# Sliding-window attention and an MLP on one core: value tiles shifted by half a block, 192 score columns per head in 64x64 tiles, row variance on ScalarE

## The chip, the core and the metric

The kernel runs on one core of a Trainium2 chip. The metric is device time in microseconds (us). The engines are TensorE (PE, its weight loads shown apart as PEld), VectorE (DVE), ScalarE (ACT), GpSimd (POOL, here mostly an issuer of DMAs) and SyncE (SP, an issuer of DMAs).

## What is computed

Eight sequences of 576 tokens with 8 heads of 64 go through causal attention with a window of 128 keys and a linear (ALiBi) bias, and the result, 512 wide, through a row normalisation, a 512 to 2048 to 512 MLP with a ReLU, and a residual add:

```python
scores = scale * np.matmul(q, k.transpose(0, 1, 3, 2))
rel = pos[:, None] - pos[None, :]
mask = (rel >= 0) & (rel < window)                    # window = 128
scores = np.where(mask, scores + bias[None], -1000000000.0)
attn = softmax(scores)
x = heads_joined(np.matmul(attn, v))                  # (8, 576, 512)
mu = np.mean(x, -1); var = np.mean((x - mu) ** 2, -1)
xn = (x - mu) / np.sqrt(var + 1e-06) * g_ln
out = x + np.maximum(xn @ w_ch1, 0.0) @ w_ch2
```

## The kernel before

The 4608 rows are 36 blocks of 128 tokens. Nine blocks make two sequences (a period); r is a block's place in its period, and i its place in the order of work. The blocks with r = 0 are i = 0, 2, 4 and 27: they have no block before them. Eleven chunks of the MLP take 2, 2, 2, 2 and then seven times 4 blocks.

For every block, `attention(i)` does this:

- **Loads.** q, k and v come by DMAs that cast to fp16, issued on POOL's queue (`load_cast`, L496; a block of 128 rows of one operand is one DMA, L551 and L553 are the weights'). The first two blocks come by SP. q and k are turned by SP's transposing DMA into `qkt` (L710), for the first nine blocks by PE (L695).
- **Scores** (`e_s`, L732). The head width of 64 uses half of PE's rows, so two heads run beside each other in 64x128 tiles, into two PSUM banks. Queries of the block meet the keys of the block before (128 columns) and of the block itself (128): 256 columns per head, 16 matmuls a block in 8 pairs, and 8 matmuls where r = 0.
- **Bias and mask.** For i below 5 PE first writes slope times distance into the bank (`e_z`, L748: the scaled identity `sid` times `dist_t`), 8 matmuls of 256 columns, or of 128 where r = 0. Later blocks multiply the exponentials with a table (`mreg`, `mmix`, `mnew`) on DVE (L787).
- **Exponential** on ACT (L780): two instructions of 1024 columns a block, 512 where r = 0.
- **Values** (`e_pv`, L808): per head a matmul of the 128x128 probabilities with the 65 columns of values and ones of the block before, and one with the block's own: 16 matmuls a block, 8 where r = 0. `pva` and `pvb` are the two halves (four heads each).
- **Rows.** DVE divides by the sum (L825, L829), takes mean and variance with bn_stats and bn_aggr (L848, L854), and scales (L868 or L892); the row is turned by PE (L906) for the first six blocks and by SP's DMA afterwards (L921, into `xt`).

The MLP's first product is `A` (L1210, weights `w1sb`), the second `B` (L1247) for the first four chunks; chunks 4 to 10 use a seven-product form of the second matrix product (`seven`, L992, `Pa` to `Pg`), and chunks 9 and 10 of the first one also (`fours`, L1121, `Ua` to `Ug`). ReLUs run on ACT (L1227) or DVE (L1225). Matmuls on `warm_t` (L1287, written ~38 in the order) only keep PE busy at the start.

The order of everything is written out by hand-over of a list: the string `ORDER` names each task with its engine (T for PE, V, A, G, S) and PSUM bank, and every engine works its tasks off in that order. The costs and due times that stand beside the tasks have no effect at run time. So when an instruction waits, all that stands behind it on its engine waits too.

Of the kernel before, what the change touches and what calls it, by code (L numbers as in the profile page):

```python
# [9 lines left out]
FP16 = mybir.dt.float16  # L10
# [46 lines left out]
class Plan:  # L57
# [22 lines left out]
    def run(self):  # L80
# [39 lines left out]
dist:G qs0.0.i:S iden1:G ks0.0.i:S dist01:G dist00:G qs1.0.i:S iden2:G sid5:V sid3:V ks1.0.i:S sid2:V sid0:V sid1:V sid4:V sid7:V sid6:V v0.i:S  # L120
iden3:V ~38 Za0:T0 Zb0:T0 cT0.00:A g.i:A cT0.10:G w0.i:G ~16 T0.0:T0 cT0.01:A q2.i:G eT0.00:V cT0.11:V k2.i:G ~8 Sa0:T0 T0.1:T1 exa0:A v1.i:G eT0.01:A
eT0.10:V Za1:T0 cv0:A G:T2 q3.i:G eT0.11:A k3.i:G Sb0:T0 Gc:A Sa1:T0 exb0:A pva0:T0 v2.i:G Gk:T1 rc0.0:V exa1:A nm0.0:V Zb1:T0 w3.i:G pvb0:T2 Sb1:T0
rc1.0:V nm1.0:V v3.i:G exb1:A mu0:V xs0:V w1.i:G ~10 T2:T0 Z2:T0 w2.i:G ev2:V pvb1:T2 pva1:T3 q5.i:G rc1.1:V S2:T0 rc0.1:V nm1.1:V TX0:T0 exb2:A
nm0.1:V q4.i:G xt0:V exa2:A ~4 T3:T2 mu1:V k4.i:G xs1:V Z3:T0 ev3:A bn1:V w4.i:G TX1:T3 pva2:T0 pvb2:T2 xt1:V S3:T0 Gkc:V rc0.2:V w5.i:G rc1.2:V
A0.0:T3 nm0.2:V exb3:A nm1.2:V w6.i:G A0.12:T1 mu2:V exa3:A xs2:V A0.14:T0 bn0:V r0.12:A r0.0:V pvb3:T2 r0.14:A Z4:T0 rc1.3:V ag0:V pva3:T1 w7.i:G
nm1.3:V A0.2:T3 rc0.3:V nm0.3:V TX2:T0 mu3:V A0.6:T2 xs3:V xt2:A A0.4:T1 r0.6:V k5.i:G bn3:V TX3:T0 r0.4:A A0.8:T2 v4.i:G bn2:V xt3:A ag1:V A0.10:T1
ag2:V k6.i:G r0.8:A A1.14:T0 q6.i:G r0.10:V r0.2:V A1.12:T2 r1.14:A ln0:A T4:T1 rs0:A r1.12:A A1.0:T3 ev4:A q7.i:G A1.4:T0 B1.0:T2 r1.4:V r1.0:V
A1.6:T1 k8.i:G S4:T0 A1.10:T0 exa4:A r1.6:A B0.0:T3 r1.10:A k8.i:G exb4:A B1.4:T2 A1.2:T1 sumT0.0:V B0.4:T3 r1.2:V q8.i:G B1.8:T2 sumT0.1:V k7.i:G
sumT0.2:V B0.8:T3 q8.i:G sumT0.3:V B1.12:T2 q9.i:G T5:T0 o1.0:V B0.12:T3 ev5:A v5.i:G sumT1.0:V pvb4:T1 B2.0:T2 o0.0:V k9.i:G mreg30:A mreg10:A
rc1.4:V mreg11:A pva4:T0 nm1.4:V S5:T0 mreg01:A k10.i:G rc0.4:V nm0.4:V B3.0:T3 exb5:A sumT1.1:V v6.i:G T6:T1 mu4:V exa5:A ag3:V xs4:V q10.i:G A1.8:T0  # L130
ev6:V mreg20:A B3.4:T3 k11.i:G mreg31:A bn4:V mreg21:A ln1:A S6:T0 mreg00:A r1.8:V v7.i:G rs1:A T8:T1 mkb5:V exb6:A dist2:G T7:T0 ev8:V B3.8:T3
q11.i:G exa6:A mka5:V pvb5:T1 q12.i:G ev7:V B2.4:T2 rc1.5:V QT9.i:S nm1.5:V v8.i:G pva5:T0 B2.8:T2 rc0.5:V nm0.5:V k12.i:G mka6:V S7:T0 v8.i:G mu5:V
B2.12:T2 mkb6:V exb7:A QT10.i:S xs5:V v9.i:G TX4:T1 exa7:A B3.12:T3 xt4:V k13.i:G mmixc:V TX5:T0 pva6:T1 o3.0:V xt5:A S8:T0 q13.i:G o2.0:V pvb6:T0
exb8:A A2.2:T3 v11.i:G mkb7:V A2.8:T2 mnewc:V r2.2:A v10.i:G QT11.i:S z2:V mka7:V A2.0:T3 r2.8:A rc1.6:V rc0.6:V z1:V A2.14:T2 r2.0:A nm1.6:V mkb8:V
exa8:A A2.12:T0 nm0.6:V sumT1.2:V pvb7:T3 r2.12:A pva7:T1 bn5:V S9:T0 r2.14:A QT12.i:S rc1.7:V A2.4:T0 z3:V exb9:A ag4:V nm1.7:V A2.10:T2 mu6:V exa9:A
xs6:V A2.6:T3 k15.i:G rc0.7:V bn6:V XT6.i:S r2.4:A mka8:V S10:T0 q15.i:G r2.6:A nm0.7:V B5.0:T0 r2.10:A mu7:V exa10:A ag6:V xs7:V pvb8:T3 pva8:T1
B5.4:T0 ag5:V exb10:A bn7:V XT7.i:S k16.i:G rc1.8:V B4.0:T2 mka9:V k15.i:G nm1.8:V QT13.i:S S11:T0 rc0.8:V dist2a:G nm0.8:V q15.i:G B4.4:T2 mkb9:V
exb11:A v13.i:G bn8:V B5.8:T0 exa11:A mkb11:V q14.i:G pvb9:T3 pva9:T1 ln2:A mka11:V B4.8:T2 rs2:A k14.i:G ag8:V rc0.9:V rc1.9:V B5.12:T0 nm0.9:V
v12.i:G ag7:V nm1.9:V ln3:A B4.12:T2 rs3:A bn9:V k17.i:G mkb10:V pvb11:T1 A3.2:T3 q16.i:G ag9:V o4.0:V ln9:A rs9:A S12:T0 r3.2:A q17.i:G xs8:V
rc1.11:V pva11:T2 o5.0:V XT8.i:S exb12:A A3.0:T3 xs9:V exa12:A A3.4:T0 nm1.11:V XT9.i:S rc0.11:V mka10:V A3.8:T1 r3.4:A nm0.11:V bn11:V A3.6:T0 r3.8:A  # L140
mkb12:V r3.0:A pvb10:T2 pva10:T1 QT14.i:S rc1.10:V S13:T0 rc0.10:V nm0.10:V A3.10:T3 exa13:A nm1.10:V out1.0.i:S bn10:V pvb12:T1 out0.0.i:S r3.6:A
A3.14:T2 ag11:V r3.10:V B6.0:T0 ag10:V r3.14:V ln11:A rs11:A exb13:A A3.12:T3 xs10:V mka13:V XT10.i:S scaleW2:A B7.0:T2 xs11:V r3.12:V B6.4:T0
XT11.i:S scaleW3:V B7.4:T2 scaleW1:A QT15.i:S B6.8:T0 rc1.12:V mkb13:V nm1.12:V B7.8:T2 k19.i:G B6.12:T0 QT16.i:S scaleW0:A v15.i:G S14:T0 o6.0:V
v14.i:G pva13:T3 mka12:V B7.12:T2 out2.0.i:S rc0.13:V exa14:A nm0.13:V pvb13:T1 pva12:T0 o7.0:V A4.8:T3 v20.i:G exb14:A rc1.13:V rc0.12:V nm1.13:V
A4.1:T2 v16.i:G nm0.12:V QT17.i:S mkb14:V S15:T0 r4.1:A v15.i:G mka14:V A4.3:T1 exb15:A bn12:V q18.i:G A4.0:T0 sumT1.3:V exa15:A k18.i:G r4.8:V
A4.10:T2 mka15:V q21.i:G S16:T0 r4.10:A r4.3:V A4.12:T3 q19.i:G exb16:A r4.0:V A4.11:T2 bn13:V q20.i:G exa16:A ag12:V r4.12:V A4.4:T1 dist1:G r4.11:A
mkb15:V k20.i:G A4.9:T0 r4.4:A ag13:V mka16:V v17.i:G ln13:A pvb14:T3 rs13:A A4.15:T2 r4.9:A xs12:V rc1.14:V XT12.i:S nm1.14:V pva14:T1 pva15:T0
rc0.14:V A4.7:T3 nm0.14:V QT18.i:S rc0.15:V nm0.15:V A4.14:T1 r4.7:A xs13:V mkb16:V A4.2:T0 out3.0.i:S bn14:V pvb15:T3 r4.2:A S17:T0 r4.15:A sa4.0:V
A4.6:T0 r4.14:A rc1.15:V sb4.0:V exb17:A A4.5:T2 XT13.i:S nm1.15:V r4.6:A A4.13:T1 bn15:V out6.0.i:S r4.5:A ag14:V sc4.0:V Pa4.00:T3 r4.13:A Pb4.00:T0
QT19.i:S exa17:A sa4.1:V Pa4.01:T3 Pb4.01:T0 ag15:V ln15:A Pa4.10:T3 out5.0.i:S rs15:A Pb4.10:T0 xs14:V out4.0.i:S Pa4.11:T3 xs15:V XT14.i:S Pb4.11:T0  # L150
sb4.1:V pvb16:T2 ra4.0:V k23.i:G pva16:T1 S18:T0 XT15.i:S rb4.0:V k21.i:G Pc4.00:T3 exb18:A Pc4.10:T3 sd4.0:V Pd4.00:T0 v24.i:G rc1.16:V exa18:A
QT20.i:S mka17:V Pc4.11:T3 Pd4.01:T0 k22.i:G rc0.16:V nm1.16:V Pc4.01:T3 mkb17:V Pd4.10:T0 v19.i:G rc4.0:V pva17:T2 Pd4.11:T0 q22.i:G nm0.16:V S19:T0
rd4.0:V Pe4.00:T3 v18.i:G exb19:A sc4.1:V Pe4.10:T3 pvb17:T1 rc0.17:V dist1a:G Pf4.10:T0 q23.i:G rc1.17:V nm0.17:V Pf4.00:T0 sd4.1:V Pe4.11:T3 q24.i:G
Pe4.01:T3 nm1.17:V Pf4.11:T0 k22.i:G QT21.i:S Pf4.01:T0 A5.0:T2 q22.i:G rf4.0:V A5.9:T1 bn17:V v23.i:G r5.0:A re4.0:V exa19:A A5.7:T0 v22.i:G mkb19:V
Pg4.00:T3 q25.i:G r5.9:V S20:T0 bn16:V Pg4.10:T3 k24.i:G exa20:A mka19:V A5.2:T2 v21.i:G mkb18:V Pg4.11:T3 QT23.i:S r5.2:A r5.7:V Pg4.01:T3 k25.i:G
pva19:T1 mka20:V A5.3:T2 rc0.19:V rg4.0:V A5.15:T0 r5.3:A nm0.19:V mka18:V A5.11:T3 r5.15:A ag17:V ag16:V exb20:A QT22.i:S A5.1:T1 r5.11:A pvb19:T2
pvb18:T0 ln17:A rc1.19:V S21:T0 nm1.19:V rs17:A r5.1:A mkb20:V A5.8:T3 xs16:V A5.10:T2 rc1.18:V r5.8:A XT16.i:S pva18:T1 r5.10:A A5.4:T3 rc0.18:V
v26.i:G out7.0.i:S exb21:A nm0.18:V xs17:V A5.14:T2 q26.i:G nm1.18:V exa21:A sa5.0:V A5.6:T1 k26.i:G QT24.i:S r5.14:A sb5.0:V A5.5:T0 r5.6:A bn18:V
r5.4:A A5.13:T2 out9.0.i:S bn19:V XT17.i:S sc5.0:V A5.12:T1 r5.13:A ag18:V mkb21:V Pa5.00:T3 r5.12:A ag19:V Pb5.00:T2 r5.5:V ln19:A S22:T0 rs19:A
sa5.1:V Pa5.01:T3 exb22:A xs19:V Pb5.01:T2 xs18:V Pa5.10:T3 sc5.1:V exa22:A Pb5.10:T2 XT19.i:S sb5.1:V Pa5.11:T3 pva20:T1 ra5.0:V pvb20:T0 XT18.i:S  # L160
# [1169 lines left out]
```

## Time and profile before

| what | us |
|---|---|
| runs shown | 302.86, 299.45, 301.07 |
| median | 301.07 |
| the profiled execution's own time | 300.98 |
| its span, first to last instruction | 299.1 |
| PE busy / DVE / ACT / POOL | 293.3 / 242.8 / 165.3 / 105.4 |
| PE's own waits in all (four) | 2.5 |
| scores L732, 544 matmuls, PE busy (all forms) | 38.2 |
| values L808, 544 matmuls, PE busy (all forms) | 30.4 |
| exponentials L780 on ACT | 67.4 |
| bn_stats L848 and bn_aggr L854 on DVE | 24.2 and 5.7 |

The profiled execution took 300.98 us, 0.09 below the median; 1.9 of it lie around the span. A matmul's time in the profile includes its way through the array (a 65-column matmul is given 193 ns), so neighbours overlap, and what a matmul costs in a row is the distance from its start to the next start.

### The profile page before, as it was taken

To read this page: it belongs to the slowest core of one execution; us is meant where nothing else is said; L and a number is where in the kernel's file an instruction comes from. 1 tells how busy PE (TensorE), PEld (TensorE's weight loads), DVE (VectorE), ACT (ScalarE), POOL (GpSimd) and SP (SyncE) were. 2 spreads that over 40 slices of the span, in tenths; PEclk is the share of its full clock that TensorE was granted. 3 is DMA by queue.
4 is the path that set the end of the run, shared out by engine and by line. 5 is a ranking of instruction groups with operands and counts; after the bars stand their busy time and mean duration, and the time that the engine had idled before them with its cause. 6 is when DMAs were issued, how large, how long until landed. Compare 5 with 4: busy or idle time off the path is not lost.

```text
span 299.1 us, 7458 instructions
## 1 busy us (share of the span) xinstructions
PE 293.3 (98%) x3014; PEld 225.1 (75%) x3014; DVE 242.8 (81%) x583; ACT 165.3 (55%) x273; POOL 105.4 (35%) x138
## 2 busy tenths in 40 slices
PE   8999999999999999899999999999999999999995
PEld 8789756875955578566886588657787799999984
DVE  3397289998879879849978888788899988988983
ACT  3664536794798573368528444676544655245500
POOL 5965369738137428433633567300000000000000
PEclk9799999999999999999999999999999999999999
DMA  6999999999999999999999999968101033012015
GB/s 179 159 196 194 206 144 141 146 138 133 122 219 145 151 224 133 145 140 167 179 166 197 182 159 143 158 171 150 36 19 55 0 125 89 2 37 106 35 55 193
DMA packets 163779, 39.93 MB, mean 133 GB/s; under 512 B 154017, under 2 KB 159137, under 8 KB 163746
## 3 DMA queue, kind: packets, MB, share of 16 engines
q0 software_dynamic: 110000, 17.70, 95.6%
q1 hardware_dynamic: 53744, 21.77, 40.5%
q8 instruction: 23, 0.38, 0.6%
q14 instruction: 10, 0.08, 0.1%
q10 hardware_dynamic: 2, 0.00, 0.0%
HBM read 36.70 MB, written 9.44 MB: 154 GB/s over the span
## 4 chain that ended last, share of the span: by engine, by line
PE 94%; DMA 4%; DVE 1%; ACT 0%; issue 0%
PE fb L1210 32%; PE fb L992 27%; PE fb L1247 9%; PE u L1121 8%; PE sc L732 6%; PE fb L808 6%; DMA qkt<-qk 4%; PE fb L1287 2%; PE sc L748 1%; PE fb L695 1%; PE fb L440 0%; PE fb L906 0%; PE fb L426 0%; DVE ot L1004 0%; DVE xb L829 0%; ACT probs L780 0%
## 5 line engine op out<-in xcount | busy, mean ns | idle before, releaser
L1210 PE MATMUL fb<-xt,w1sb 128*128 128x512 f16 (+1 forms) x576 | 106.4, 332 | 0.6 <-DMA xt<-xs 0.6
L780 ACT ACTIVATE probs<-sc 128x1024 f16<-128x1024 f32 (+1 forms) x72 | 67.4, 975 | 36.0 <-PE sc L732 27.3
L1210 PEld LDWEIGHTS <-w1sb 128*128 128x128 f16 x576 | 61.5, 114 | 27.8 <-DMA xt<-xs 0.9
L1227 ACT ACTIVATE ht<-fb 128x512 f16<-128x512 f32 x88 | 51.1, 598 | 44.4 <-PE fb L1210 44.2
L992 PEld LDWEIGHTS <-ht 128*128 128x128 f16 x560 | 53.2, 98 | 9.2
L496 POOL DMA_DIRECT2D qk<-in_k_dram x38 | 32.8, 866 | 44.3 <-DMA qkt<-qk 36.8
L992 PE MATMUL fb<-w2sb,ht 128*128 128x256 f16 x336 | 44.7, 273 | 0.0
L496 POOL DMA_DIRECT2D qk<-in_q_dram x38 | 32.5, 861 | 16.6 <-DMA qkt<-qk 9.6
L496 POOL DMA_DIRECT2D vx<-in_v_dram x36 | 31.0, 868 | 15.6 <-PE fb L808 12.4
L787 DVE TENSOR_TENSOR probs<-probs,mreg 128x1024 f16<-128x1024 f16 (+1 forms) x46 | 30.4, 667 | 1.1 <-ACT probs L780 1.0
L992 PE MATMUL fb<-ks,ht 128*128 128x256 f16 x224 | 30.8, 273 | 0.0
L1247 PE MATMUL fb<-w2sb,ht 128*128 128x512 f16 x128 | 30.7, 379 | 0.0
L829 DVE SCALAR_TENSOR_TENSOR xb<-fb,rec 128x256 f16<-128x256 f32 x72 | 29.5, 416 | 0.9
L808 PEld LDWEIGHTS <-probs 128*128 128x128 f16 x544 | 23.9, 98 | 6.8
L808 PE MATMUL fb<-vx,probs 128*128 128x65 f16 x496 | 26.1, 194 | 0.0
L1004 DVE TENSOR_TENSOR ot<-fb,xb 128x512 f32<-128x512 f32 (+1 forms) x31 | 19.6, 634 | 6.0 <-PE fb L992 5.6
L848 DVE BATCH_NORM_STATS2 st<-xb 128x6 f32<-128x512 f16 x36 | 24.2, 682 | 0.2
L825 DVE RECIPROCAL rec<-fb 128x4 f32<-128x4 f32 x72 | 12.2, 174 | 14.7 <-PE fb L808 12.4
L1225 DVE TENSOR_SCALAR ht<-fb 128x512 f16<-128x512 f32 x24 | 16.0, 681 | 8.4 <-PE fb L1210 8.3
L1247 PEld LDWEIGHTS <-ht 128*128 128x128 f16 x128 | 11.6, 98 | 11.1
L732 PEld LDWEIGHTS <-qkt 64*128 64x128 f16 x496 | 14.9, 94 | 6.4 <-issue 5.3
L1144 DVE TENSOR_TENSOR ht<-u,probs 128x512 f16<-128x512 f32 x24 | 16.2, 685 | 2.7 <-PE u L1121 1.8
(113 smaller groups left out, 387.7 us busy)
## 6 DMA issues: line engine op xcount, KB each, us to landing
out_dram<-ot SPq DMA_DIRECT2D x32, 256.0 KB, 2.9
qk<-in_q_dram POOLq DMA_DIRECT2D x30, 128.0 KB, 7.6
qk<-in_k_dram POOLq DMA_DIRECT2D x30, 128.0 KB, 7.2
vx<-in_v_dram POOLq DMA_DIRECT2D x28, 128.0 KB, 7.7
w1sb<-in_moe_w_ch_dram POOLq DMA_DIRECT2D x4, 512.0 KB, 9.1
w2sb<-in_moe_w_ch_dram POOLq DMA_DIRECT2D x4, 512.0 KB, 14.1
out_dram<-ot SPq DMA_DIRECT2D x8, 128.0 KB, 1.8
qs<-in_q_dram SPq DMA_DIRECT2D x2, 256.0 KB, 3.6
```

The costliest lines, as they stand in the source:

```text
L496: nc.gpsimd.dma_start(out=dst(p0, n), in_=src[b, :, s0 : s0 + n, :].rearrange("h p d -> p h d"))
L732: nc.tensor.matmul(scs[half][:, g, c0 : c0 + P], kt[rows, 1, hp, :], qkt[i][rows, 0, hp, :], start=not bias, stop=True, skip_group_check=True,
L780: nc.scalar.activation(out=o, in_=n_, func=AF.Exp, scale=inv_sqrt_d)
L787: en.tensor_tensor(out=pv, in0=pv, in1=mask[:, 2 * half : 2 * half + 2, :, lo:], op=ALU.mult)
L808: nc.tensor.matmul(pp[:, hh * (D + 1) : hh * (D + 1) + D + 1], probs[i][:, bank, slot, side * P : side * P + P], vx[i if side else before] ...
L829: nc.vector.scalar_tensor_tensor(out=xb[c][:, j, 256 * half : 256 * half + 256].rearrange("p (h d) -> p h d", d=D), in0=pp[:, :, 0:D], sca ...
L848: nc.vector.bn_stats(out=st[i][:, :], in_=xb[c][:, j, :])
L992: nc.tensor.matmul(o, lhs(f, p), rhs(f), start=first and f == 0 and (p == 0 or key[0] != key[1]), stop=f == F2 - 1, skip_group_check=True)
L1121: nc.tensor.matmul(late[bank][:, FOURTH * f : FOURTH * f + FOURTH], w, rhs[kb], start=first and f == kb == 0, stop=kb == 1, skip_group_che ...
L1210: nc.tensor.matmul(fb[b][:, n_ * x : n_ * x + n_], w1f[f // CB][:, kb, (f + x) % CB, :], xt[c][:, kb, 0:n_], start=(kb == x == 0), stop=(k ...
L1227: nc.scalar.activation(out=o, in_=src, func=AF.Relu)
L1247: nc.tensor.matmul(pm[:, 0 : c1 - c0], ht[c][:, f, j * P : j * P + P], w2sb[f // CB][:, f % CB, c0:c1], start=(f == 0), stop=(f == NFB - 1),)
```

## The change

1. **Value tiles shifted by half a block.** A tile of values now holds the 128 tokens that begin half a block before the queries' block. A query block then needs three pieces of keys: a near tile of 128 keys that all its queries use, and two outer pieces of 64 keys, each used by 64 queries. The score columns per head are 128 + 64 = 192. `load_v` loads tiles in halves where a block's half is not there yet: 42 v transfers on POOL's queue in place of 39, two on SP in place of one, of the same bytes in all. The ring of value tiles has 8 + 6 in place of 9 + 3.
2. **64x64 tiles.** Scores: for each pair of heads four matmuls of 128 columns and four of 64 columns, each with 64 keys as weights and 64 PSUM partitions as target. Where r = 0, two and two. Values: `pw` does the two outer pieces for all heads (16 matmuls, 64 rows by 64 targets, into the two halves of the partitions of one bank), then `pva` and `pvb` do the near tile (4 each, 128x128). `pw` needs the exponentials of both halves.
3. **Bias by matmul** has 192 columns for all blocks, and block i = 27 (r = 0) takes it too instead of a mask. `dist_t` gets a fourth table; POOL makes the tables at the start in 11 steps (before: 3), two of them after the first loads.
4. **Exponentials** 768 columns for every block; masks 768 columns.
5. **Variance.** bn_stats and bn_aggr go. DVE sums each row while dividing (accumulator for all blocks, before for the first 8), makes minus the mean (`mu`, now 36), and ACT squares x - mean with an accumulator (`sq`, 36).
6. **`ORDER` anew.** Among others: PE's `pw` mostly stands beside a score task; of the ReLUs L1225 and L1227, DVE has 45 in place of 24 and ACT 67 in place of 88; 65 matmuls on `warm_t` in place of 76; the weights w3, w1, w2 are issued behind 12 other transfers of POOL (before: w3 behind 7); the first A task follows the scores and values of blocks 0 to 3 and the scores of block 4 (before: the scores of blocks 0 to 3).

```diff
-                        for side in (() if r == 0 else (0,)) + (1,):
-                            for g in range(2):
-                                rows = slice(D * g, D * g + D)
-                                kt = qkt[i if side else before]
-                                c0 = slot * 2 * P + side * P
-                                nc.tensor.matmul(scs[half][:, g, c0 : c0 + P], kt[rows, 1, hp, :], qkt[i][rows, 0, hp, :], ...)
+                        near_ = [(own, lower, upper, 0, 0, P)] + ([(ago, upper, lower, 0, 0, P)] if r else [])
+                        outer_ = [(own, upper, lower, P, HALF, HALF)] + ([(ago, lower, upper, P, 0, HALF)] if r else [])
+                        for g, (kt, keys, to, col, q0, n) in [(g, x) for some in (near_, outer_) for g in range(2) for x in some]:
+                            rows = slice(D * g, D * g + D)
+                            nc.tensor.matmul(scs[half][to, g, c0 + col : c0 + col + n], kt[rows, 1, hp, keys], qkt[i][rows, 0, hp, q0 : q0 + n], ...)
...
-                                scs[half][:, g, slot * 2 * P + lo : slot * 2 * P + 2 * P], sid[:, h, :], dist_t[:, kind, lo:],
+                                scs[half][:, g, slot * W3 : slot * W3 + W3], sid[:, h, :], dist_t[:, kind, :],
...
+        def e_pw(e, b):
+            pr_ = by_head(probs[i])
+            for half in range(2):
+                pp = fb[plan.held[f"V{'ab'[half]}{i}"][1]]
+                for hh in range(4):
+                    h = 4 * half + hh
+                    bank, slot = 2 * half + h % 2, hh // 2
+                    for rows, q_, vt in ((lower, upper, v_after), (upper, lower, v_ago)):
+                        nc.tensor.matmul(pp[q_, hh * (D + 1) : hh * (D + 1) + D + 1], pr_[rows, bank, slot, outer],
+                            vx[VT[vt]][rows, h, 0 : D + 1], start=hh == 0, stop=True, skip_group_check=True)
...
-                    for side in (() if r == 0 else (0,)) + (1,):
-                        nc.tensor.matmul(pp[...], probs[i][:, bank, slot, side * P : side * P + P], vx[i if side else before][:, h, 0 : D + 1], ...)
+                    nc.tensor.matmul(pp[...], pr_[:, bank, slot, near], vx[VT[v_near]][:, h, 0 : D + 1], start=False, ...)
...
-            nc.vector.bn_stats(out=st[i][:, :], in_=xb[c][:, j, :])
-            nc.vector.bn_aggr(out=mv[c][:, j, :], in_=st[i][:, :])
+            nc.scalar.activation(out=squares[:, :], in_=xb[c][:, j, :], func=AF.Square, bias=mean[i][:, 0:1], accum_out=mv[c][:, j : j + 1])
```

More of the change, by code (lines that the diff above doesn't have):

```diff
@@ L124 @@
[L124 to L127, printed above, removed]
@@ L391 @@
         nc.vector.memset(t[:, :, D:VD], 1.0)
+    for n in range(HEADS):
+        nc.vector.memset(vx[VT[n, 0]][0:HALF, :, 0:D], 0.0)
     far = 16000.0
@@ L461, in emit @@
                 )
-            tm.append(add(f"mreg{bank}{slot}", ("ACT", 0.4), emit, d_dist[0], av(MASK_AT, 0.0)))
+            tm.append(add(f"mreg{bank}{slot}", ("ACT", 0.35), emit, d_dist[0], av(MASK_AT, 0.0)))
     tmix, tnew = [], []
@@ L798, in attention @@
         fast = c >= SEVEN
+        n_pair = BLOCK[i] // PERIOD
+        v_near, v_after, v_ago = ((n_pair, r + d) for d in (0, 1, -1 if r else 0))
+        def e_pw(e, b):
[6 more added lines that the diff above has]
+                    for rows, q_, vt in ((lower, upper, v_after), (upper, lower, v_ago)):
+                        nc.tensor.matmul(
+                            pp[q_, hh * (D + 1) : hh * (D + 1) + D + 1],
+                            pr_[rows, bank, slot, outer],
+                            vx[VT[vt]][rows, h, 0 : D + 1],
+                            start=hh == 0,
+                            stop=True,
+                            skip_group_check=True,
+                        )
+        pw = add(f"pw{i}", ("PE", 0.25), e_pw, pr + v_done[v_after, 0] + v_done[v_ago, 1], av(i, 5.0), lat=0.0, acq=[("fb", f"V{x}{i}") for x in "ab"])
+        probs.reads(i, pw)
+        for t in (v_after, v_ago):
+            vx.reads(VT[t], pw)
         for half in range(2):
@@ L835, in e_nm @@
                     op1=ALU.mult,
-                    accum_out=None if fast else sums[i][:, half : half + 1],
+                    accum_out=sums[i][:, half : half + 1],
                 )
@@ L839, in attention @@
             rec.writes(2 * i + half, rc)
-            n_ = add(f"nm{half}.{i}", ("DVE", 0.48), e_nm, [rc], av(i, 5.2 + half), rel=key)
-            if not fast:
-                sums.writes(i, n_)
+            n_ = add(f"nm{half}.{i}", ("DVE", 0.52), e_nm, [rc], av(i, 5.2 + half), rel=key)
+            sums.writes(i, n_)
             rec.reads(2 * i + half, n_)
@@ L1065, in seven @@
                     t, d = plan.transfer(f"out{i}.{cols.start}", "SP", 0.42, 0.8 * (cols.stop - cols.start) / d_model, 0.12, e_d, deps, v0 + (4 * n + 4) * step - 4.0)
-                    ot.reads(k0 + half, d)
+                    ot.reads(k0 + half * (NP - 1), d)
     def first_sums():
-        free = [t for r_ in (probs, qkt) for ts_ in r_.readers.values() for t in ts_] + masked
-        wsums["free"] = free
         for m in range(2):
@@ L1087, in pick1, with tile_reads @@
         return Choice(default, cost)
+    def tile_reads(ring_, n):
+        return [t for k, ts in ring_.readers.items() if k not in ring_.pins and ring_.turn(k) % len(ring_.tiles) == n for t in ts]
     def fours(c, done, v0, room):
@@ L1198, in mlp @@
             return
-        order = [x for n in range(NFB // 2) for x in (n, n + NFB // 2)] if fast else range(NFB)
+        order = [x for n in range(NFB // 2) for x in (n, n + NFB // 2)] if fast and nb == CB else [x for n in range(0, NFB // 2, 2) for x in (n, n + 1, n + NFB // 2, n + NFB // 2 + 1)] if fast else range(NFB)
         two = 2 if nb == 2 else 1
```

491 lines of the change are left out of this document (264 added, 227 removed).

## The prediction

> **What bounds the kernel now.** I read the page's busy shares first, then the list of PE's waits, then busy time by stage, and last the order of time around one block's attention.
>
> ```profile
> PE 293.3 (98%) x3014; PEld 225.1 (75%) x3014; DVE 242.8 (81%) x583; ACT 165.3 (55%) x273; POOL 105.4 (35%) x138
> ```
>
> ```profile
> PE fb L1287 <- DVE warm_t L387: 1.1, 1, 1.1
> PE fb L1210 <- DMA xt<-xs: 0.6, 1, 0.6
> PE sc L732 <- DMA qkt<-qk: 0.5, 1, 0.5
> PE fb L1287 <- DVE xb L829: 0.3, 1, 0.3
> ```
>
> ```profile
> 0.00:20.00 20.00, 18.48 (x234) 15.80 (x235) 9.67 (x53) 10.25 (x15) 14.65 (x26) 0.91 1.37 175
> 20.00:110.00 90.00, 90.00 (x947) 64.46 (x946) 73.72 (x185) 62.55 (x104) 47.64 (x60) 1.00 2.07 162
> 110.00:130.00 20.00, 18.91 (x207) 14.22 (x206) 16.84 (x36) 6.71 (x9) 13.00 (x18) 1.00 2.19 155
> 130.00:210.00 80.00, 80.00 (x833) 56.27 (x832) 66.31 (x158) 47.68 (x77) 30.10 (x37) 1.00 1.68 164
> 210.00:296.00 86.00, 85.91 (x801) 74.32 (x798) 75.93 (x155) 38.08 (x70) 0.00 (x0) 1.00 0.20 60
> ```
>
> PE is the bound and has hardly a hole: its waits add up to 2.5 us, and after the first 20 us it lacks work only in the stage 110 to 130, by 1.1 us, both times for a transposing DMA. It waits for DVE only while the start runs, and for ACT never. So what the change takes from ACT and DVE is worth nothing by itself; only matmul time, the changes of PE's tile shape, the start and the DMA waits count. What they cost is read from starts:
>
> ```profile
> 60.21 0.65 PE L808 MATMUL fb<-vx,probs 128*128 128x65 f16 x16
> 60.78 0.23 PE L732 MATMUL sc<-qkt,qkt 64*128 64x128 f16 x2
> 60.85 0.22 PE L732 MATMUL sc<-qkt 64*128 64x128 f16 x2
> 60.91 0.22 PE L732 MATMUL sc<-qkt,qkt 64*128 64x128 f16 x2
> 60.96 0.22 PE L732 MATMUL sc<-qkt 64*128 64x128 f16 x2
> 61.02 0.22 PE L732 MATMUL sc<-qkt,qkt 64*128 64x128 f16 x2
> 61.07 0.22 PE L732 MATMUL sc<-qkt 64*128 64x128 f16 x2
> 61.13 0.22 PE L732 MATMUL sc<-qkt,qkt 64*128 64x128 f16 x2
> 61.19 0.22 PE L732 MATMUL sc<-qkt 64*128 64x128 f16 x2
> 61.34 0.41 PE L1210 MATMUL fb<-xt,w1sb 128*128 128x256 f16 x2
> ```
>
> Sixteen value matmuls cover 0.65 us, the last one 0.19 of it, so one follows another after (0.65 - 0.19) / 15 = 0.030 us. The last starts at 60.67 and the scores at 60.78: 0.11 in place of 0.03, about 0.09 too long. A pair of score matmuls follows the last after 0.056 us ((61.19 - 60.85) / 6). From the last pair to the next product are 0.15 us, again 0.09 more than 0.056. So a visit to the half-height tiles costs 0.19 us beside its matmuls.
>
> **The change part by part.** The sum is made against the profiled execution's 300.98 us, 0.09 below the median of the runs.
>
> Scores. In a block with r above 0, 8 rounds of 128 columns (8 x 0.056 = 0.448) become 4 rounds of 128 and 4 of 64, each of four matmuls side by side. The trace shows no matmul that writes 64 targets and no four at once. Bounds: four at once cost no more than two do, and a round of 64 columns takes what the value matmul of 65 columns takes, 0.030, so 4 x (0.056 + 0.030) = 0.344; or nothing is gained over pairs, 8 x 0.056 + 8 x 0.030 = 0.688. I take the first, because in the rows above two row halves already work side by side at the price of one. 32 blocks x 0.104 = -3.3 us. Where r = 0, 4 rounds of 0.056 become 4 to 4 x 0.086; I take no change (at most 4 x 0.12 = +0.5).
>
> Values. With r above 0, 16 x 0.030 = 0.48 become 8 near matmuls (0.24) and 8 pairs of outer ones (0.24 if a pair costs one): nothing. The four blocks with r = 0 go from 8 x 0.030 to 0.48: 4 x 0.24 = +1.0. If pairs do not overlap, 36 x 0.24 = +8.6 (a rival below).
>
> Bias matmuls. L748's rows at 14.89 (8 of 128 columns in 0.61 us) and 17.59 (4 of 256 in 0.60) give 0.056 and 0.109 from start to start, so 192 columns lie at 0.082. Before 3 x 8 x 0.056 + 2 x 8 x 0.109 = 3.1 us, after 6 x 8 x 0.082 = 3.9: +0.8.
>
> Changes of tile shape. Counted along the two orders, PE goes into the smaller tiles 37 times before and 44 times after, since most outer value tasks stand next to a score task: 7 x 0.19 = +1.3. If every one stood alone it would be 36 x 0.19 = 6.8.
>
> ACT and DVE. Exponentials: 1023 ns at 1024 columns (64) and 594 at 512 (8) give 809 at 768, so 72 x 0.809 = 58.2 for 67.4. Twenty-one ReLUs leave at 598 ns (-12.6). The square is not in the trace: the nearest row, an ACTIVATE of 512 fp16 elements, takes 626 ns; with DVE's accumulator read of 82 ns on top 0.71, so 36 x 0.63 to 36 x 0.8 = 23 to 29 us. ACT goes to about 167 to 173 us of 299. DVE loses 24.2 + 5.7 (statistics) and 8 (masks: 62 of up to 679 become 60 of 548 ns), gains 28 x 0.210 (means), 56 x 0.082 (accumulators) and 21 x 0.681 (ReLUs): 13 less. All this lies beside PE's matmuls; cost nothing. Were that cover gone, a square that waits for its mean would hold the exponentials behind it on ACT, and through the score banks PE's next scores; but along the new order at least 6.5 us of matmuls lie between scores and their outer value task from block 4 on, against 2 x 0.81 + 2 x 0.55 = 2.7 us of exponentials and masks.
>
> DMAs. Three more value issues on POOL at 0.87 us, same bytes; POOL is 35% busy and waits 46.3 us for q and k tiles to come free, so they are hidden, apart from the start.
>
> The start. PE's first A matmul begins at 19.6 us. The matmuls that stand ahead of it make 14.9 us at full speed, so 4.7 went to waits and to the clock (0.91 over the first 20 us, 1.8 us lost). In the new order 16.8 us stand ahead of the first A, because block 4's turn, bias and scores and block 3's outer values moved forward; with the same 4.7 it begins at 21.5, no loss, as that work is done. Eleven warm-up matmuls fewer are 11 x 0.056 = -0.6. Bounds: the half-clock stretch does not come (-1.8), or a weight comes late (+2.8, a rival below).
>
> The DMA waits of 1.1 us: the transposes of chunk 5's rows are now issued 6.7 us of matmuls ahead of use in place of 8.2, block 21's q and k 14.8 in place of 10.5; one gets worse, one better. No change, bounds -1.1 and +1.5.
>
> Sum: -3.3 + 1.0 + 0.8 + 1.3 - 0.6 = -0.8, so 300.98 - 0.8 = **300.2 us**: the matmul time saved in the scores is given back by four blocks' values, the bias and the tile changes.
>
> **The rivals.**
>
> *The small tiles' weights are not hidden: slower.* Each score block issues 32 weight loads for 0.344 us of matmuls, 16 before for 0.448. Where matmuls are too short to hide a load, the trace shows its price:
>
> ```profile
> 10.41 0.74 PEld L440 LDWEIGHTS fb<-ot 1*128 1x128 f32 x6
> 10.41 0.82 PE L440 MATMUL fb<-ot 1*128 1x1 f32 x6
> ```
>
> one-column matmuls and their loads follow each other after (0.74 - 0.19) / 5 = 0.11 us (the last load itself takes 0.19): 128 columns of fp32 weights. 64 such columns are 0.055 us. At this price a 64-column round costs 0.055, so scores fall back to 0.444 (+3.2) and the outer values to 8 x 0.055 = 0.44 (+0.20 x 36 = 7.2): 310.6. With two bytes a weight loading in half the time, but the two tiles of a row half one after the other, only the scores lose: 303.4. It decides as soon as four loads take longer than 0.030 us. For: no row has a 64-column weight. Against: 128 fp16 columns are hidden behind each 0.030 us value matmul. The Trainium skill, TensorEngine Tiling (Array Packing), section Restrictions, says that column tiling switches the fast weight load off. By that rule the hidden loads of the value rows would not carry over to the new tiles; no run yet shows it. Chance 0.22.
>
> *Outer value pairs do not overlap.* The two matmuls of a pair write the same PSUM bank, in different partitions; the score pairs above write two banks. One after the other they cost 16 x 0.030, +8.6: 308.8. The Trainium skill, same page, section Gotcha 1: PSUM Pressure, says that different row tiles can't access one bank at the same time; the trace has no such pair. Chance 0.10.
>
> *The start and the DMA waits fall well.* No half-clock stretch (-1.8) or no DMA wait in the middle (-1.1): 298.4 with the first, 297.3 with both. For: both hang on moments that the new order shifts. Against: PE still idles while first loads land. Chance 0.22.
>
> *w3 comes late: slower.* POOL issues 12 transfers at 0.87 us ahead of w3, from about 5.5 us on: 16.0, plus the 9.1 us that a w1sb transfer takes to land (median), is 25.1; the second A task needs it at 21.5 + 0.9 = 22.4. +2.8: 303.0. Against: the quickest of the four took 5.8 us, then it is there at 21.8. Chance 0.10.
>
> **How the numbers follow.** The forecast keeps 0.36, as 300.2 with its own range 298.5 to 302.5 (the DMA and r = 0 bounds). A measurement here can tell about 1% from no change: 298.1 and 304.1. Faster: nearly all of the third rival's 0.22 and a little of the forecast's, 0.22. Slower: the second rival, the first's dearer half and a part of combinations, 0.28. Within 1%: 0.50. The range of 8 in 10 runs from 297.0 to 309.0.
>
> **What would show it.** In the profile after: the distance from one block's first score to the next product (0.34 + 0.15 if four tiles overlap, 0.45 or more if weights bound); the 16 outer value matmuls in 0.24 or in 0.48 us; PE's waits still under 4 us in all; the first A near 21.5 us with w3 landed by 22.4; DVE about 229 us busy and ACT about 170 without any change of the time for it. The prediction is wrong if PE waits for ACT or DVE after the start, or if a 64-wide tile costs other than the 128-wide rows suggest.

## The result, and the profile after

The changed kernel is about 1% slower. The first comparison gave 305.05 us against 300.95 for the kernel before, ratio 1.0132 (95% interval 1.0092 to 1.0172); a second one, e1, with seven executions for four, 303.93 against 300.84, ratio 1.0092 (1.0060 to 1.0123). The forecast was 300.2. Ratios leave out disturbed executions, such as the profiled one of the first comparison (377.09 us at a granted clock of 0.76), medians do not; all readings of "after" below are from e1's profile: 303.75 us, span 302.0.

The busy shares of the changed kernel:

```profile
PE 294.7 (98%) x3875; PEld 224.4 (74%) x3875; DVE 229.2 (76%) x620; ACT 168.4 (56%) x323; POOL 108.0 (36%) x148
```

DVE and ACT came out where they were forecast (229, and 167 to 173), and PE is as full as it was. The new forms on ACT, in the list of the costliest groups (count, busy time, mean ns of one, then the idle time before them):

```profile
L824 ACT ACTIVATE probs<-sc 128x768 f16<-128x768 f32 x72 | 55.5, 805 | 33.7 <-PE sc L779 22.8 <-PE fb L874 11.0
L918 ACT ACTIVATE squares<-xb,mean 128x512 f16<-128x512 f16 x36 | 25.9, 721 | 14.1 <-DVE mean L911 13.0 <-DVE rec L889 0.9
L918 ACT ACTIVATION_READ_ACCUMULATOR squares<-xb,mean 128x1 f32 x36 | 6.9, 193 | 0.0
```

An exponential was forecast at 809 ns and takes 805; the square, bounded by 0.63 and 0.8 us, takes 0.72 and 0.19 more to read its sum, so 0.91 in all. The list of PE's waits (us in total, times, longest) has new names behind its first, which is the one that `warm_t` had before:

```profile
PE fb L1346 <- DVE squares L399: 1.1, 1, 1.1
PE fb L1051 <- DVE ot L1063: 1.0, 1, 1.0
PE fb L1269 <- DVE ot L1314: 0.9, 1, 0.9
PE fb L742 <- DMA qk<-in_q_dram: 0.4, 1, 0.4
PE sc L779 <- ACT qktp L752: 0.2, 1, 0.2
PE fb L1269 <- DMA w1sb<-in_moe_w_ch_dram: 0.2, 1, 0.2
```

Both waits of the stage 110 to 130 are gone. One of about 1 us has come in the stage before it and one near 210, as busy time by stage shows (start and end, length, then PE busy; the granted clock is the third number from the end):

```profile
0.00:20.00 20.00, 17.84 (x294) 14.68 (x295) 9.37 (x53) 10.99 (x15) 17.74 (x36) 1.00 1.53 168
20.00:110.00 90.00, 88.96 (x1270) 62.99 (x1269) 65.43 (x187) 61.42 (x121) 47.89 (x59) 1.00 1.76 163
110.00:130.00 20.00, 20.00 (x245) 15.11 (x244) 16.44 (x42) 9.54 (x21) 10.31 (x13) 1.00 1.94 157
210.00:296.00 86.00, 85.06 (x844) 72.97 (x844) 74.60 (x164) 40.34 (x80) 0.00 (x0) 1.00 0.23 63
```

One block's attention in the order of time (start, length):

```profile
118.18 0.24 PE L779 MATMUL sc<-qkt 64*64 64x128 f16 x1
...
118.55 0.43 PE L854 MATMUL fb<-vx,probs 64*64 64x65 f16 x16
118.91 0.61 PE L1051 MATMUL fb<-qs,qs 128*128 128x256 f16 x4
```

From the first score to the first outer value matmul are 0.37 us, from there to the next product 0.36. Neither the weights' price (0.444) nor values one after the other (0.48) is to be seen.

**Where the time went.** Distances from start to start of PE's tasks, summed over both profiles, give this account; what a task takes over the median of its kind, beyond 0.06 us, is put down as a wait:

| us, from start to start | before | after | difference |
|---|---|---|---|
| scores and values | 37.8 | 36.4 | -1.4 |
| the MLP's matmuls (19 of these tasks stand ahead of a small tile before, 35 after, 0.095 each) | 236.6 | 237.9 | +1.3 |
| bias matmuls | 3.2 | 4.7 | +1.5 |
| warm-ups | 6.5 | 6.0 | -0.5 |
| turns of q, k and rows, and gains | 8.0 | 8.5 | +0.5 |
| waits | 2.1 | 3.7 | +1.6 |
| last matmul's start | 295.64 | 298.59 | +2.95 |

In this execution half of the loss is waits and half is work: the small tiles save nothing net and the bias costs more. The forecast had -1.0 for the first two rows together, +0.8 for the bias, -0.6 for the warm-ups and no waits.

**The two new stops.** The stop at 209.7 can be followed through DVE's and SP's rows:

```profile
183.79 20.44 SPq L757 DMA_TRANSPOSE qkt<-qk  x4
204.33 2.86 SPq L978 DMA_TRANSPOSE xt<-xs  x2
```

```profile
208.89 0.41 DVE L949 TENSOR_SCALAR xs<-xb,mean,rstd 128x512 f16<-128x512 f16 x1 [1.12 <-DMA xt<-xs]
...
210.20 0.69 DVE L1063 TENSOR_TENSOR ot<-fb,xb 128x512 f32<-128x512 f32 x1 [0.42 <-DMA out_dram<-ot]
```

The four transposes of the first line end with block 34's. SP can issue that one only at 203.0, because its k lands at 202.9, and is done with it at 204.3; behind it stand the transposes of rows 24 and 25. DVE's next row waits 1.12 us for a buffer that such a transpose still reads (there are three). Behind that row stands `ra7` (L1063), which has to empty PE's bank. So a load on POOL reaches PE through SP and DVE, and PE's list names only the last link.

The other stop is named after DVE, wrongly:

```profile
64.68 4.05 SPq L978 DMA_TRANSPOSE xt<-xs  x2
```

```profile
76.55 1.04 PE L1269 MATMUL fb<-xt,w1sb 128*128 128x256 f16 x8 [0.86 <-DVE ot L1314]
```

The DVE operation that ends just ahead of it comes later in `ORDER`, so this task can't wait for it. It reads block 7's row, whose transpose went out at 67.1 and took 9.3 us: 76.4.

### The profile page after: what moved, and what is told of

Read it like the earlier page. It is cut to its first block, busy times and chain, and to the rows that moved or that the text cites. A ratio compares the mean times of both kernels' runs of the same rounds, so it can differ in the third digit from the quotient of the medians.

```text
span 375.3 us, 9298 instructions
## 1 busy us (share of the span) xinstructions
PE 370.3 (99%) x3875; PEld 250.1 (67%) x3875; DVE 233.7 (62%) x620; ACT 170.1 (45%) x323; POOL 107.9 (29%) x148
## 4 chain that ended last, share of the span: by engine, by line
PE 94%; POOL 2%; DMA 2%; issue 0%; ACT 0%; DVE 0%; POOLq 0%
PE fb L1269 34%; PE fb L1051 30%; PE fb L1306 10%; PE u L1180 8%; PE sc L779 4%; PE fb L874 3%; PE fb L854 3%; DMA qk<-in_q_dram 2%; PE fb L742 1%; POOL qk L517 1%; PE fb L963 0%; PE sc L795 0%; POOL vxp L554 0%; ACT qktp L752 0%; POOL w1sb L609 0%
## 5 line engine op out<-in xcount | busy, mean ns | idle before, releaser
L1269 PE MATMUL fb<-xt,w1sb 128*128 128x512 f16 (+1 forms) x576 | 134.8, 397 | 0.0
L824 ACT ACTIVATE probs<-sc 128x768 f16<-128x768 f32 x72 | 55.5, 806 | 51.5 <-PE sc L779 35.2
L1286 ACT ACTIVATE ht<-fb 128x512 f16<-128x512 f32 x67 | 39.4, 596 | 59.1 <-PE fb L1269 58.7
L1051 PE MATMUL fb<-w2sb,ht 128*128 128x256 f16 x336 | 55.9, 319 | 0.0
L1284 DVE TENSOR_SCALAR ht<-fb 128x512 f16<-128x512 f32 x45 | 30.7, 688 | 36.6 <-PE fb L1269 36.5
L918 ACT ACTIVATE squares<-xb,mean 128x512 f16<-128x512 f16 x36 | 25.9, 719 | 18.2 <-DVE mean L911 16.7
L1063 DVE TENSOR_TENSOR ot<-fb,xb 128x512 f32<-128x512 f32 (+1 forms) x31 | 19.5, 638 | 14.7 <-PE fb L1051 14.5
L832 DVE TENSOR_TENSOR probs<-probs,mreg 128x768 f16<-128x768 f16 x44 | 23.8, 556 | 6.9 <-ACT probs L824 6.8
L1193 ACT ACTIVATE probs<-u 128x512 f32<-128x512 f32 x21 | 12.2, 596 | 26.4 <-PE u L1180 20.2
L1063 DVE TENSOR_TENSOR ot<-fb,ot 128x512 f32<-128x512 f32 (+1 forms) x22 | 14.6, 665 | 14.9 <-PE fb L1051 14.8
L779 PEld LDWEIGHTS <-qkt 64*64 64x64 f16 x992 | 15.9, 111 | 8.1 <-issue 7.3
```

Source lines behind the costliest of these rows:

```text
L779: nc.tensor.matmul(scs[half][to, g, c0 + col : c0 + col + n], kt[rows, 1, hp, keys], qkt[i][rows, 0, hp, q0 : q0 + n], start=not bias, sto ...
L824: nc.scalar.activation(out=o, in_=n_, func=AF.Exp, scale=inv_sqrt_d)
L1051: nc.tensor.matmul(o, lhs(f, p), rhs(f), start=first and f == 0 and (p == 0 or key[0] != key[p]), stop=f == F2 - 1, skip_group_check=True)
L1063: nc.vector.tensor_tensor(out=out[:, p0:p1], in0=src, in1=in1[:, p0:p1], op=ALU.add)
L1269: nc.tensor.matmul(fb[b][:, n_ * x : n_ * x + n_], w1f[f // CB][:, kb, (f + x) % CB, :], xt[c][:, kb, 0:n_], start=(kb == x == 0), stop=(k ...
L1284: nc.vector.tensor_scalar(out=o, in0=src, scalar1=0.0, scalar2=None, op0=ALU.max)
```

## The experiments

Theory A: the miss is the price of the matmuls. Theory B: it is in the queues, transposes and loads that come late. Theory C came up on the way: PE runs short of instructions. Runs that name the same time for the kernel before share its executions. A block count of 31 in two expectations is 30 (block 27 is not doubled).

**e1: the changed kernel again.** No edit.

> The changed kernel once more, unchanged, for a profile at full clock. Theory A (matmul time): the score blocks cost more than 0.344 us or the changes of tile shape more than 0.19 us a visit, so that PE's time after the first 20 us grows by some 4 us without any wait. Theory B (start): the first A matmul begins later than the 21.5 us of the forecast, by 2 to 4 us, and the rest is as forecast. Theory C (DMA waits): PE's listed waits after 20 us add up to 3 us or more, against 1.1 us before. About 304 us in each case.

Result above: A and B each have a part.

**e2: the transposes of rows ahead of those of q and k.**

```diff
-... QT32.i:S ... QT33.i:S ... QT34.i:S ... XT24.i:S ... XT25.i:S ...
+... QT32.i:S ... XT24.i:S ... XT25.i:S QT33.i:S QT34.i:S ...
```

> The changed kernel, but on SP's queue the q and k transposes of blocks 33 and 34 stand behind the row transposes of blocks 24 and 25 and not ahead of them; nothing else moves. Theory B (the miss is in queues): the stop of 1.15 us at 209.7 is a chain: PE waits for DVE's ra7, which stands behind xs, which waits for a buffer that a row transpose still reads, and that transpose stood on SP behind two transposes whose q and k had not landed. Then the stop goes and the time falls by 0.9 to 1.2 us, to 302.8. Rival: the row transposes were late by their own transfers and the next wait of DVE takes the place of this one; the time falls by less than 0.4 us, 303.5 to 304. Theory A (the miss is matmul time) says nothing of this run beyond that the other 2 us stay.

303.18 us against 300.31, 1.0083 (1.0052 to 1.0114). The profiled execution took 301.52 us and has neither stop; block 7's transpose landed 8.2 us after its issue there. One execution without a stop proves little, since e14, of the unedited kernel, has none either. The traces together support the chain: the stop is in none of the seven profiled executions with this order (e2, e7, e10, e11, e15, e16, e18). Of the old order, e1, e13 and e17 have it, with block 34's k landing at 202.9, 201.5 and 202.1 us, and e14 has not, where it landed at 198.4; e6, e8 and e9, whose PE work differs, have none either. The median cannot tell 0.7 us from none, because its executions spread from 301.5 to 304.7, with one at 311.6.

**e3 and e4: the scores issued twice, after and before.**

```diff
-                for half in halves:
+                for half in halves * (1 if bias else 2):
```

> The changed kernel with the score matmuls of the 31 masked blocks with r above 0 issued twice into the same places (the output stays the same). Each block pays the price of its scores once more, without a change of tile shape. Trace price, from the distances of the run above: 0.371 us, 31 x 0.371 = 11.5, 315.4 us. The forecast's price of 0.344: 10.7, 314.6. Rival, weights bound the narrow rounds: 0.444 or more, 13.8, 317.7 or more.

> The kernel before with the same doubling of its 31 masked blocks with r above 0 (output the same): 31 x 0.448 = 13.9, 314.7 us. The difference of the two additions is what the new tiles gain in the scores of these blocks: by the forecast 31 x 0.104 = 3.2 us, by the trace 31 x 0.077 = 2.4 us, and nothing if weights bound the narrow rounds.

e4: 313.6 us against 300.31, 13.3 more; in its trace the doubled blocks take 1.000 where 0.553 stood, so 0.447 a block. e3: 325.94 (321.7 to 328.6), 22 more than e1, far beyond every price. Its trace parts the two causes. Where nothing interferes a doubled block takes 0.721 in place of 0.371 (or 0.824 in place of 0.474 when it leaves the small tiles): the scores cost 0.350, 0.097 less than before, and the forecast's 0.344 was right. The rest is stops of a new name:

```profile
PE sc L779 <- issue: 7.5, 4, 2.5
PE fb L1269 <- issue: 2.7, 2, 2.4
```

```profile
69.14 0.20 PE L779 MATMUL sc<-qkt 64*64 64x64 f16 x2
71.86 0.21 PE L779 MATMUL sc<-qkt,qkt 64*64 64x64 f16 x1 [2.52 <-issue]
```

In the middle of a score task, which waits for nothing, PE stands for 2.7 us. These stops begin ahead of matmuls 990, 1118 and 1246 of the program, 128 apart; with the weight loads that is 256 instructions. A 16 KB transfer on the queue for instructions ends at 63.2, 70.1 and 77.4 us, and PE goes on at 64.8, 71.9 and 78.9.

**e5: the variance on DVE again.**

```diff
-            nc.scalar.activation(out=squares[:, :], in_=xb[c][:, j, :], func=AF.Square, bias=mean[i][:, 0:1], accum_out=mv[c][:, j : j + 1])
+            nc.vector.bn_stats(out=st[i][:, :], in_=xb[c][:, j, :])
+            nc.vector.bn_aggr(out=mv[c][:, j, :], in_=st[i][:, :])
```

> The changed kernel with one part undone: the variance comes from bn_stats and bn_aggr on DVE again, at the places in the order where the squares stood; ACT loses 36 x 0.9 = 33 us, DVE gains 36 x 0.83 = 30 us (229 to about 259, 86% of the span). Theory A and the forecast (ACT and DVE work lies beside the matmuls, its price is nothing): 303.9 within 0.6. Rival (DVE's queue already carries the two stops of the profile, at 75.3 and 209.7, and more work on it makes them longer and adds others): 305 to 308.

311.28 us, 7.4 above e1 (1.0355 to the kernel before, 1.0300 to 1.0411) and above the rival's 308. DVE is 82% busy, about as full as it was before the change (81%), and PE now waits in many places:

```profile
PE sc L780 <- DMA qkt<-qk: 1.8, 1, 1.8
PE fb L1271 <- DMA xt<-xs: 1.1, 2, 0.7
...
PE fb L1053 <- DVE ot L1065: 0.7, 2, 0.4
PE fb L1053 <- DVE ht L1286: 0.7, 1, 0.7
PE fb L1271 <- DVE ht L1286: 0.5, 2, 0.3
```

So DVE's work is not free in this order. It lies beside PE's work only as long as the order was laid for it. PE waits for late results of DVE themselves (`ot`, `ht`) and for transposes of late rows (`xt`); what made the transpose of q and k late (1.8) was not followed.

**e6: half of three in four outer pairs left out** (the oldest keys are missing for three heads in four).

```diff
-                    for rows, q_, vt in ((lower, upper, v_after), (upper, lower, v_ago)):
+                    for rows, q_, vt in ((lower, upper, v_after), (upper, lower, v_ago))[: 1 if hh else 2]:
```

> The changed kernel, its outer value task (16 matmuls of 64x64) leaving out the second matmul of three of the four pairs per half: 10 matmuls in place of 16, so the oldest keys are missing for three heads in four. If the two matmuls of a pair run beside each other, as the distances of 0.249 us per task say, the time stays: 303.9 within 0.6. If they run one after the other (the second rival of the forecast), 36 x 6 x 0.030 = 6.5 us go: 297.4.

304.31 us, no gain where 6.5 us were at stake. In its trace a task of 10 matmuls takes 0.351 us to the next product, one of 16 took 0.361: the two matmuls of a pair, which write one bank, overlap.

**e7: row 7 earlier.** e2, and `z3` and `mka9` behind `xs7` on DVE, `pvb7` ahead of `A2.4` on PE.

> The changed kernel with the order of e2 and, beside it, on DVE the clearing of the mnew table and the mask mka9 behind xs7, and on PE pvb7 ahead of A2.4: the row of block 7 is ready up to 1 us earlier, and its transpose (9.3 us from issue to landing in the first run, 8.2 in e2) can go as soon as the one before it is issued. Theory B: the stop of 1.03 us at 75.3 is the landing of this transpose, the profile's name for it (a DVE operation that comes later in the order) is wrong; then it is gone in nearly all executions, the times of this kernel no longer fall into two groups about 2 us apart, and the median is 301.8 to 302.3. Rival (DVE's own o4 and o5 hold it): 303.2 as in e2.

303.17 us against 300.72, 1.0073 (1.0047 to 1.0099). The profiled execution (301.7) has no stop after the start, but the others spread from 301.6 to 305.1, with two at 307.0 and 308.9. The expected median failed.

**e8: more visits to the small tiles.** (The task now also waits for its near value tile.)

```diff
+                if half == 0:
+                    nc.tensor.matmul(pp[:, 0 : D + 1], pr_[:, 0, 0, near], vx[VT[v_near]][:, 0, 0 : D + 1], start=True, ...)
```

> The changed kernel with one 128x128 matmul of 65 columns put ahead of each outer value task, into a bank that the task then clears (output the same). 20 of the 36 outer tasks stand right behind other 64x64 matmuls, so PE leaves the small tiles and enters them again 20 times more. Theory (a visit costs about 0.20 us, 0.09 to 0.11 at each end): 36 x 0.030 + 20 x 0.20 = 5.1, 309.0 us. Rival (the distances at the ends of a visit are no price of the tile change): 36 x 0.030 = 1.1, 305.0.

308.77 us, 4.8 more than e1: (4.8 - 1.1) / 20 = 0.19 for a visit. Single executions differ by more than a microsecond, so this is good to about 0.05, but the rows agree: leaving the small tiles takes 0.122 and entering them again 0.133, in place of 0.02 from small tile to small tile, so 0.20 a visit beside the 0.03 of the added matmul. PE enters the small tiles 37 times before the change, 44 times after it and 64 times here. The forecast's price and its count hold.

**e9: as much PE time in six instructions.**

```diff
+                for x in range(0 if bias else 3):
+                    nc.tensor.matmul(scs[x % 2][:, 0, 0 : 2 * P], iden[:, :], sid[:, 0:2, :], start=True, ...)
```

> A counterpart of e3, which took 22 us in place of 10.7 for the doubled scores: the changed kernel with three 128x128 matmuls of 256 columns ahead of the scores of the same 30 blocks, into places that the scores overwrite (output the same). PE is held longer by the same 0.33 us a block, but by 6 instructions and not by 64. Theory C (in e3 PE ran out of instructions: its stops begin 128 matmuls, 256 instructions, apart and end about 1.5 us after a transfer of 16 KB on the queue for instructions): 30 x 3 x 0.109 = 9.8, and 11 more tile changes x 0.20 = 2.2, 316 us, and no stop above 1 us inside the scores. Rival (whatever delays the exponentials by 0.35 us a block starts a chain of waits): 322 or more, with stops as in e3.

314.43 us, 10.5 more than e1, and no stop after the first 17 us (e1's own two stops are not there either, so the added work is nearer the 12 of the expectation). So e3's stops are not those of late exponentials; they come with the number of instructions.

**e10, e11, e12: the first weights later on POOL's queue.**

```diff
-... w0.i:G ... k2.i:G ... q2.i:G ... k3.i:G ... q3.i:G ...
+... k2.i:G ... q2.i:G ... k3.i:G ... q3.i:G w0.i:G ...
```

> The kernel of e7, but on POOL's queue the first weights w0 (wanted by the first A task near 22.5 us) stand behind q and k of blocks 2 and 3 and the values of block 1, not ahead of them. Theory: at the start PE waits for q of block 3 because a weight transfer that is wanted 5 us later is ahead of it (waits of 0.31 and 0.60 us in the first run, 1.1 in e7, and the scores of block 3 behind them); then these waits go, first A near 21.5, and the time is 0.8 to 1.5 us below e7: 301.7 to 302.4. Rival: w0 now lands too late for the first A, or the later weights do, and the wait only moves: 303.2, or up to 304.5.

> As e10, with w0 two issues further back, behind the values of block 2 and k of block 4. If the early transfers share one stream, w0 lands about 1.5 us later than in e10, near 21 to 22.5 us: the waits for q and k are gone as in e10, and the first A begins to wait for w0 by up to 1 us: 302 to 303. Rival (the stream is not the limit): the same time as e10 within 0.3.

> The kernel before with the same single move: w0 behind q and k of block 3 on POOL's queue. It tells whether what e10 mends is a fault of the new order or one that both kernels have. PE waits 0.4 us before its third turn at 16.4 and 0.3 more before that; its first A stands at 19.6 us, 3 us earlier than in the new order, so w0 has less room: 300.2 to 300.9 if both effects are small, 301.5 to 303 if w0 becomes late.

The first two are e7's kernel with this move. 305.38, 304.71 and 301.10 us against 300.89: e10 lies above even its rival's 304.5, and e11 meets neither of its expectations. The last, 1.0021 (1.0001 to 1.0041), says that the kernel before has nothing to gain there either. In e10 the third turn begins at 16.7 in place of 17.6 (e7), but the first A at 22.8 and A2.0 at 57.5 as in e7: the wait moved on, as the rival said (in e11 into 1.6 us for values, before the outer values of block 2). Then PE stops for instructions at matmuls 990 and 1117, where e7 did not:

```profile
76.90 0.38 PE L1269 MATMUL fb<-xt,w1sb 128*128 128x256 f16 x2
78.89 0.85 PE L1269 MATMUL fb<-xt,w1sb 128*128 128x256 f16 x6 [1.61 <-issue]
```

The 16 KB that it needs landed at 77.4; in e7 at 74.1, with PE at matmul 1068.

**e13 to e16: more profiled executions** of the changed kernel (twice), of e7 and of e10.

> The changed kernel once more, for another profiled execution. Theory C for the change itself: between 57 and 83 us PE uses up 128 matmuls (16 KB of instructions) in 7.3 to 8.1 us, before the change in 10 to 11, and a stop at matmul 990 or 1117 named issue shows in some executions, 1 to 3 us in all, where the time is 304 or more. Theory B: such executions hold the stop of the transposes at matmul 1115 (75 us) and the one at 210 us, about 1 us each, and no stop named issue.

> As e13: another profiled execution of the changed kernel; a stop named issue at matmul 990 or 1117 (theory C), or stops at 75 and 210 us behind transposes only (theory B).

> Another profiled execution of e7, whose median stayed at 303.2 while its profiled execution took 301.7 with no stop after the start. If this one takes 303 or more, it shows what the slower executions hold: theory C a stop named issue at matmul 990 or 1117, theory B a stop of PE for a transpose; with 302 or less neither.

> Another profiled execution of e10 (all its six times 303.5 to 306.5). Theory C: the stops at matmul 990 and 1117 named issue (1.2 and 1.9 us in e10) come again, within 1 us; rival: they were chance, this execution has none and takes 302.

The changed kernel: 302.92 us with the stop at 210 alone, 301.57 with neither, beside e1's 303.75 with both; the list names none of PE's waits issue in any of the three. That is theory B for the large stops. Theory C is close at hand: in e14 PE stands for 0.27 us ahead of matmul 1117, in the middle of a task, until 1.6 us after the 16 KB landed. In e14 the last matmul starts at 296.41, so without the late stops the changed kernel is still 0.8 us behind the kernel before (295.64). e7 again: 305.03, with waits for the first k (1.3), for block 7's row (1.2), for weights at the start (1.1) and for instructions at matmul 990 (0.4). e10 again: 304.62, with 1.6 for the first k and 1.3 for values at the start, and the same two places near 70 and 77 us (0.3 for instructions, 1.0 for the row). In both, block 7's transpose landed (78.83 and 78.42 us) 0.13 us before PE went on, as in e1; the instructions had landed at 77.5 and 77.1.

**e17 and e18: the first k ahead of the first values on SP, alone and on top of e7.**

```diff
-... v0.i:S ... ks1.0.i:S ... v0.i:S ...
+... ks1.0.i:S v0.i:S ... v0.i:S ...
```

> The changed kernel with one move on SP: the second half of the first k (heads 4 to 7) is loaded ahead of the first values, as before the change, and not behind them. In its four profiled executions PE's second turn waits 0.2 to 1.6 us for the cast of this load, in the one of the kernel before 0.3. Theory B (waits at the start): the cast ends 0.7 us sooner or more, Za1 to T0.1 is shorter by it, and the time falls by 0.3 to 1.0 us. Rival: the start is bound by the loads of q and k behind it (PE waits for q of block 3 at 16.4 us anyway), the wait moves there: 303.9 within 0.4 of the run before.

> The kernel of e7 (both stops behind transposes taken away) with the move of e17 as well: the best version that these runs point to. Theory B alone: 300.7 to 302.0, level with the kernel before. Theory C (stops for instructions and the first loads come and go from one execution to the next): a median of 302.3 to 303.2, single executions from 300.5 to 305, no faster than before.

303.57 us against 300.43, 1.0092 (1.0067 to 1.0118), and 303.66, 1.0109 (1.0082 to 1.0137); e18 is above both of its expectations. In e17's profile A2.0 begins 0.8 us earlier than in e1 (56.64 for 57.40), and 20 us later PE stops 0.9 us for instructions that landed at 74.4, no sooner than in e1:

```profile
PE fb L1051 <- DVE ot L1063: 1.2, 1, 1.2
...
PE fb L1269 <- issue: 0.9, 1, 0.9
```

What PE gains at the start it loses, in this execution, where its instructions come no faster. No mended version is told apart from the changed kernel by its interval, and none reaches the kernel before.

## Why the prediction was wrong, by its own steps

The time came out above the forecast's own range (298.5 to 302.5), on the slower side, and by none of the rivals' ways. Of the 3.7 us between the forecast of -0.8 and the account's +2.95, 1.6 are waits that the forecast put at nothing, and 2.1 are terms of work that were too small or left out.

- **Scores, -3.3: right.** 0.350 in place of 0.344, so 32 x 0.097 = -3.1 (e3, e4). Four small tiles at once cost no more than two did, and 64 columns little more than the 65 of a value matmul. The first rival (weights) falls with it. The Trainium skill, TensorEngine Tiling (Array Packing), section Restrictions, has column tiling switch the fast weight load off; at these sizes (0.350 us measured, 0.344 forecast) no cost of it is seen.
- **Changes of tile shape, +1.3: right.** 0.19 a visit (e8), and 37 and 44 entries in the traces.
- **Values, +1.0: mis-sized, +2.1.** A block with r above 0 takes 0.249 + 2 x 0.130 = 0.51 in place of 2 x 0.244 = 0.49: 32 x 0.021 = +0.7. The step from scores to outer values costs another 0.021, 19 times: +0.4. The four blocks with r = 0 are +1.0 as forecast. The second rival falls: 16 matmuls, in pairs that write one bank, take 0.249 us, and leaving six of them out gains nothing (e6).
- **Bias, +0.8: mis-sized, +1.5.** The pitch of 192 columns is 0.083 as forecast. Some 0.5 more are entries into the small tiles, already in the term above, and 0.3 is a task that now runs at the half pace of the start (0.64 in place of 0.33). Before, such a task (0.83 in place of 0.45) stands in the table as a wait; counted alike, the bias is some +1.2 and the waits +1.9.
- **ACT and DVE, 0: right for the sum, wrong in its reason.** The busy totals came as worked out, though the square alone (0.91) lies above its bound of 0.8. But "worth nothing by itself" does not hold: giving DVE 24 us of it back costs 7.4 (e5). And the forecast's own sign of being wrong, that PE waits for DVE after the start, came: 1.0 us for `ra7` at 209.7. The cover was named between scores and values; what failed in e1 is the rows' way through their transposes, in both stops.
- **Start, -0.6, and DMA waits, 0: this is the step that failed.** Warm-ups gave -0.5. Waits over 0.1 us went from 0.8 to 1.5 in the first 30 us and from 1.4 to 2.2 after. The first A begins at 22.55, not 21.5. I looked only at the two waits that the profile of before shows; both went, and new ones came at places where it shows none. They could have been asked for: the order of SP's queue alone has the transposes of blocks 33 and 34 ahead of rows 24 and 25, and three row buffers behind them. The bounds (-1.8 to +2.8 and -1.1 to +1.5) held these sizes; the middle of them was not zero. Turns and gains, +0.5, had no term at all.
- **w3 late, +2.8: only a trace of it.** w3 landed at 23.05, ahead of its A task at 23.43; another w1sb transfer cost 0.2 us at 28 us, and in e15 such waits are 1.1.
- **Start and waits fall well: its conditions came, its time did not.** The stretch of 3.4 us at a granted clock of 0.5, from 11.1 to 14.5 us before, is not there after (1.00 over the first 20 us, before 0.91), and the two waits of the middle are gone. Yet the first A is a microsecond late: PE is busy for 17.84 of the first 20 us in place of 18.48, and the half pace of the first matmuls, which ended at 4.3 us, still holds at 5.4. That stretch is no mark of the order either: e4, which starts as the kernel before does, has none.

In the sum, in microseconds: -3.1 + 2.1 + 1.3 for attention, +1.0 for the bias without its entries, -0.5 for warm-ups and +0.5 for turns and gains (PE waits for the first k in them) are +1.3, by the account +1.4, where -0.8 was forecast; with +1.6 of waits, where nothing was, they make the 2.95.

What stays open: what the slower executions of e7 and e18 hold one by one (e15 has four kinds of wait), and so how the waits of the median execution divide among the start, the transposes and the instructions. No run has the waits of the start taken away.

## What to carry to other kernels

When PE is full and the order of all queues is written by hand, count a new order's waits as a cost of their own: list for each queue what stands ahead of each transfer and whether its input can be there, and give the waits a middle above zero. A saving in columns by smaller tiles has to pay for entries and extra pieces, and it uses up instructions faster (3875 matmuls for 3014); here three microseconds of scores were paid back in full. An engine that is 80% busy was hidden only by the order made for it (e5).

## What the runs showed of the hardware

PE's instructions come through the DMA engines in blocks, and a kernel can use them up faster than they come. The page's list of DMA queues (transfers, MB, share) after and before:

```profile
q8 instruction: 30, 0.49, 0.7%
```

```profile
q8 instruction: 23, 0.38, 0.6%
```

After the change the transfers come 7.3 us apart around 70 us, before 9.7 to 10.9. In e3, where 128 matmuls are used up in 7 us, and in e10, e11 and e17, where a block landed with PE at most 12 matmuls ahead of needing it, PE stands for 0.3 to 2.7 us and goes on 1.3 to 1.8 us after the transfer's end. The Trainium skill, Runtime: NRT & Kernel Launch, section Instruction fetch mechanics, gives the block as 16 KiB or 256 instructions and calls the cost of crossing into the next one mostly hidden. The trace bears out the size (16 KB transfers, stops 128 matmuls and 128 weight loads apart); the cost is not hidden in these runs.

After two of e3's three stops of 2.7 us, those at 76.2 and 217.8 us, six and five matmuls of 512 columns ran at 0.427 us from start to start in place of 0.216, from 2.0 and 0.4 us after the stop. The granted clock is 0.53 from 80.5 to 84 us and 0.50 from 220.5 to 223.5. So a stop can cost more than its length.
